# Retention attention and a gated feed-forward in one kernel: sums, casts, loads, stores and quarter products in another order

## The chip, the cores and the metric

The kernel runs on one core of a Trainium2 chip. The core has a matrix engine (TensorE, PE in the profile, with PEld for its weight loads), three engines for element-wise work (VectorE or DVE, ScalarE or ACT, GpSimd or POOL), and SyncE (SP), whose queue issues almost all transfers here. Each engine runs its own queue of instructions in the order in which the program wrote them; between engines they wait for each other by semaphores. The metric is the device time of one execution in microseconds (us). The kernel of before took 303.46 us, the median of 3 runs from 302.69 to 303.69.

## The reference

Inputs are q, k and v of 8 batches, 8 heads, 576 positions and 64 elements, and three weights of a feed-forward from 512 to 1536 and back. All are float32.

```python
gamma = 1.0 - 2.0 ** (-5.0 - np.arange(H))
Dmat = np.where(rel >= 0, gamma[:, None, None] ** rel[None, :, :], 0.0)   # rel = pos[:, None] - pos[None, :]
scores = scale * np.matmul(q, k.transpose(0, 1, 3, 2))
attn = np.matmul(scores * Dmat[None], v)
x = attn.transpose(0, 2, 1, 3).reshape(B * S, H * D)                      # 4608 tokens of 512
gate = 1.0 / (1.0 + np.exp(-(x @ w_gate)))
val = x @ w_val
out = gate * val @ w_out
```

The decay in Dmat allows the attention to be computed in pieces of 128 positions: within a piece by scores and a mask, and from earlier pieces through a state of 64 by 64 per head.

## The kernel before, in words

**Stages.** The 4608 tokens are the columns of a transposed activation `xT`. They are cut into blocks: 512 columns, two blocks of 256, and seven of 512, from column 1024 to column 4096. While the feed-forward of one block runs, the attention that makes the next blocks' columns is woven in, step by step. There are some 26 attention steps. Step s has loads of k, q and v (`load`, line 165, on SP), casts with decay tables to bf16 (`cast_qk`, `cast_v`, lines 420 to 445, on POOL, ACT or DVE; `SCALED_V`, `K_ON_POOL`, `V_ON_ACT` choose), a transposing DMA from SBUF to SBUF (`cross`, line 446, on SP) that makes the tile `T` of the step, and the products on PE (`row`, `new`, `val`, lines 686 to 734). Before PE's result `val` is cast into `xT`, a short read of it (`glance`, lines 753 and 755, on ACT or DVE by `LOOK_ACT`) makes the engine wait for it.

**How loads are ordered.** `casts_to(x)` first calls `loads_to(x + AHEAD[x])`, then writes the casts of step x and its transposing DMA. `AHEAD` thus sets how many steps' loads stand ahead of the transpose in SP's queue.

**Feed-forward of the first three blocks.** The first 512 columns and the two blocks of 256 use plain products: 128 columns of a weight by up to 512 columns of `xT`. Some of them are given to PE in two halves of 256 columns: how many is set by `CUTS` (line 1359), `FIRST_OP_CUTS` (line 1539) and `OP_CUTS` (line 1297).

**Feed-forward from column 1024 on.** Each block multiplies a 2 by 2 arrangement by seven products instead of eight (Strassen's scheme in Winograd's form), once for the gate (g), once for the value (w) and for each of three thirds u of the 1536 columns. A name such as `w14` means kind w, third u = 1, product i = 4. One product is four matmuls of 128 by 256. It needs sums of weights (`wgt`, `wvt`, `wvt_last` and so on; `w_sums`, line 359, `wo_sums`, line 318) and sums of tokens (`xsum`, four per block; `x_sums`, line 959). Its results leave PSUM through `quarter` (line 1052): product 1 is copied by ACT into `gateg`/`wg`, onto which product 2 is accumulated, products 5 and 6 into `gs`/`ws` and `gu`/`wu`, to which DVE adds products 7 and 3 (lines 1088 and 1085), and each finished quarter is made into `gv`, by the sigmoid on ACT for the gate, by a multiplication on DVE or POOL for the value (lines 1071 and 1073). Each kind and third has three PSUM buffers, a, g and e (in the profile `gatea`, `gateg`, `gatee`, `wa`, `wg`, `we`), which other thirds use again in turn; `BANKS`, line 1005, says which. The down projection is done by seven products too (`quarters`, line 1140, results `qa`, `qe`, `qf`); it needs sums of `gv`, called `gsum` (`gv_sum`, line 938).

**What sets the order.** The schedule is written out by hand. The strings `FIRST` (column 1024), `ORDER` (1536 to 3584, five blocks) and `FINAL` (4096) give the order of the quarter products on PE, and with it that of their followers on ACT, DVE and POOL. A suffix `:1-1v` behind a product says that at this place a `gsum` is written, on DVE (v) or POOL (p). `LATER_FIRST`, `LATER` and `LATER_FINAL` do the same at numbered places of the down projection. `X_LATE` says which engine makes each of the four `xsum` of a block from column 1536 on (the order is xsum_0 first half, xsum_1 first half, xsum_0 second half, xsum_1 second half, which product 4 reads). `SUMS_AT` does the same for the weight sums and the casts of the first stages: `2.12:w12p` writes the sum for w, third 1, number 2 on POOL at place 12 of block 2; a `c` is a cast step. `SOONER` and `CASTS_AT` place three stores and two cast steps in block 2.

The block at column 1024 has a special end: its last third of the value is done with plain products (`value`, line 1098, `h`, line 1106), the first of each in two halves.

## Time and profile before

| what | value |
|---|---|
| median of 3 runs | 303.46 us (302.69 to 303.69) |
| the profiled execution | 303.89 us |
| its span in the trace | 302.2 us |
| granted TensorE clock, mean | 0.999 |
| DMA packets | 146464, 54.99 MB |

The span is the part that the trace shows; 1.7 us lie around it. PE starts its first real products near 12 us and its last near 298 us. Before lie loads, casts and transposes; after, the last results are copied by DVE and stored.

The share of the span by which an engine is busy is in the page's first part. The chain that ended last is followed back from the last instruction: at each step to what released it, or to the instruction ahead of it on its engine. In a timeline row stand the start in us, the duration in us, engine, line, operation, output and inputs, shape and type, and in brackets the engine's idle time before it with what ended it. PE's rows are recorded from the issue of a matmul to the modelled end of its pipeline, so neighbours overlap: the distance between starts is what a product costs PE, 0.436 us for four matmuls of 128 by 256.

### The profile page before, as it was taken

To read this page: it belongs to the slowest core of one execution; us is meant where nothing else is said; L and a number is where in the kernel's file an instruction comes from. 1 tells how busy PE (TensorE), PEld (TensorE's weight loads), DVE (VectorE), ACT (ScalarE), POOL (GpSimd) and SP (SyncE) were. 2 spreads that over 40 slices of the span, in tenths; PEclk is the share of its full clock that TensorE was granted. 3 is DMA by queue.
4 is the path that set the end of the run, shared out by engine and by line. 5 is a ranking of instruction groups with operands and counts; after the bars stand their busy time and mean duration, and the time that the engine had idled before them with its cause. 6 is when DMAs were issued, how large, how long until landed. Compare 5 with 4: busy or idle time off the path is not lost.

```text
span 302.2 us, 10696 instructions
## 1 busy us (share of the span) xinstructions
PE 295.6 (98%) x4437; PEld 250.0 (83%) x4437; DVE 230.4 (76%) x439; ACT 204.9 (68%) x414; POOL 225.8 (75%) x253
## 2 busy tenths in 40 slices
PE   7999999999999999999999999999999999999994
PEld 3677876978868888888888888888888888888883
DVE  5967895796986998789748974896489848935893
ACT  6755565335369657985798589857985698559830
POOL 5775854846669888978997898789978946860780
PEclk9999999999999999999999999999999999999999
DMA  7999999979998989999749967976694165004013
GB/s 205 336 370 379 322 334 229 210 160 202 213 175 184 257 173 196 219 201 262 141 108 199 259 143 155 218 185 143 124 204 132 37 123 193 4 2 139 3 36 104
DMA packets 146464, 54.99 MB, mean 182 GB/s; under 512 B 124400, under 2 KB 139760, under 8 KB 146416
## 3 DMA queue, kind: packets, MB, share of 16 engines
q1 hardware_dynamic: 145328, 53.59, 73.6%
q8 instruction: 34, 0.56, 0.8%
q10 hardware_dynamic: 1088, 0.72, 0.8%
q14 instruction: 14, 0.11, 0.1%
HBM read 37.75 MB, written 9.44 MB: 156 GB/s over the span
## 4 chain that ended last, share of the span: by engine, by line
PE 92%; DVE 2%; DMA 2%; issue 1%; ACT 1%; POOL 0%; SPq 0%; DVEq 0%
PE gatea L1046 12%; PE wa L1046 11%; PE qa L1173 11%; PE qe L1173 9%; PE gatee L1046 6%; PE we L1046 5%; PE op L1549 4%; PE h_v L886 3%; PE h_g L886 3%; PE gateg L1046 3%; PE wg L1046 3%; PE hv L1374 3%; PE op L1306 3%; PE val L718 2%; PE qa L1249 2%; PE hg L1374 2%
## 5 line engine op out<-in xcount | busy, mean ns | idle before, releaser
L1046 PEld LDWEIGHTS <-wg_sb 128*128 128x128 bf16 x348 | 34.1, 98 | 4.1
L1073 POOL TENSOR_TENSOR gv<-gv,wu 128x512 bf16<-128x512 bf16 x20 | 23.5, 1174 | 15.5 <-DVE wu L1085 15.4
L1173 PEld LDWEIGHTS <-gsum 128*128 128x128 bf16 x312 | 30.0, 98 | 3.7
L429 POOL TENSOR_TENSOR qk<-q,qtab 128x512 bf16<-128x512 f32 x28 | 30.3, 1082 | 3.5 <-DMA q<-in_q_dram 3.5
L1046 PEld LDWEIGHTS <-wv_sb 128*128 128x128 bf16 x296 | 28.9, 98 | 3.6 <-issue 0.2
L1085 DVE TENSOR_TENSOR gu<-gatee,gu 128x512 f32<-128x512 f32 x22 | 15.2, 690 | 19.4 <-ACT gateg L1077 10.2
L943 POOL TENSOR_TENSOR gsum<-gsum,gv 128x256 bf16<-128x256 bf16 (+1 forms) x20 | 17.6, 890 | 14.4 <-DVE gsum L943 12.6
L1046 PEld LDWEIGHTS <-wgt_sb 128*128 128x128 bf16 x264 | 25.8, 98 | 3.0
L1046 PE MATMUL gatea<-xsum,wg_sb 128*128 128x256 bf16 x172 | 25.6, 273 | 0.0
L1173 PEld LDWEIGHTS <-gv 128*128 128x128 bf16 x228 | 21.8, 98 | 2.7
L1088 DVE TENSOR_TENSOR gs<-gatea,gs 128x512 f32<-128x512 f32 x22 | 15.2, 689 | 9.5 <-PE gatea L1046 9.4
L943 POOL TENSOR_TENSOR gsum<-gv,gsum 128x256 bf16<-128x256 bf16 (+1 forms) x24 | 21.9, 922 | 0.2
L429 POOL TENSOR_TENSOR qk<-k,ktab 128x512 bf16<-128x512 f32 x11 | 11.6, 1054 | 13.4 <-DMA k<-in_k_dram 13.2
L704 DVE TENSOR_TENSOR pt<-row,tri 128x512 bf16<-128x512 f32 x30 | 19.2, 680 | 2.8 <-PE row L686 2.6
L442 POOL TENSOR_TENSOR v<-v,ktab 128x512 bf16<-128x512 f32 x19 | 20.9, 1101 | 0.0
L1046 PE MATMUL wa<-xsum,wv_sb 128*128 128x256 bf16 x136 | 20.4, 273 | 0.1
L658 ACT CAST sb<-s 128x512 bf16<-128x512 f32 (+1 forms) x26 | 14.3, 569 | 8.8 <-DVE s L829 8.7
L788 ACT CAST xT<-val 128x512 bf16<-128x512 f32 x26 | 14.7, 592 | 7.0 <-PE val L734 7.0
L943 DVE TENSOR_TENSOR gsum<-gv 128x512 bf16<-128x512 bf16 (+1 forms) x34 | 19.1, 589 | 0.0
L1046 PEld LDWEIGHTS <-wvt 128*128 128x128 bf16 x168 | 16.4, 98 | 1.9
L943 POOL TENSOR_TENSOR gsum<-gv 128x256 bf16<-128x256 bf16 (+1 forms) x20 | 17.6, 882 | 0.0
L1071 ACT ACTIVATE gv<-gs 128x512 bf16<-128x512 f32 x22 | 13.9, 633 | 5.4 <-DVE gs L1088 5.4
(210 smaller groups left out, 883.9 us busy)
## 6 DMA issues: line engine op xcount, KB each, us to landing
k<-in_k_dram SPq DMA_DIRECT2D x26, 256.0 KB, 3.9
q<-in_q_dram SPq DMA_DIRECT2D x26, 256.0 KB, 4.2
v<-in_v_dram SPq DMA_DIRECT2D x26, 256.0 KB, 4.6
out_dram<-ob SPq DMA_DIRECT2D x24, 256.0 KB, 2.7
wg<-in_moe_w_gate_dram SPq DMA_DIRECT2D x12, 256.0 KB, 5.4
wv<-in_moe_w_val_dram SPq DMA_DIRECT2D x12, 256.0 KB, 5.6
wo<-in_moe_w_out_dram SPq DMA_DIRECT2D x12, 256.0 KB, 5.6
v32p<-in_v_dram SPq DMA_DIRECT2D x6, 256.0 KB, 4.5
```

The source lines that it names most:

```text
L429: eng.tensor_tensor(out=to, in0=by_halves(loaded[s][1 - i]), in1=tab, op=ALU.mult)
L442: nc.gpsimd.tensor_tensor(out=natural["v", s], in0=loaded[s][2], in1=tab, op=ALU.mult)
L704: nc.vector.tensor_tensor(out=t[:, y, 0:n].rearrange("p i m t -> p (i m) t"), in0=rows_tile[ss[0]][y][:, 0:n].rearrange("p i m t -> p (i m ...
L788: nc.scalar.copy(out=to, in_=src)
L886: nc.tensor.matmul(ps[:, i], lhsT=w_sb[:, kc, (fc + i) * P:(fc + i + 1) * P], rhs=xT(kc, slice(t0, t0 + n)), start=(kc == 0), stop=(kc == ...
L943: eng.tensor_tensor(out=to, in0=a, in1=b, op=op)
L1046: nc.tensor.matmul(ps[:, f], lhsT=w[:, kc, f * P:(f + 1) * P], rhs=x[:, kc], start=(first and f == 0 and kc == 0), stop=(f == 1 and kc == ...
L1073: eng.tensor_tensor(out=to, in0=to, in1=src[:, part], op=ALU.mult)
L1085: nc.vector.tensor_tensor(out=me["u2"], in0=e, in1=me["u2"], op=ALU.add)
L1088: nc.vector.tensor_tensor(out=me["s5"], in0=a, in1=me["s5"], op=ALU.add)
L1173: nc.tensor.matmul(ps[:, b], lhsT=left(fp)[:, b * P:(b + 1) * P], rhs=right(fp), start=(first and fp == 0 and b == 0), stop=(fp == NFC // ...
L1374: nc.tensor.matmul(ps[:, cols], lhsT=(wg_sb if what == "g" else wv_sb)[:, kc, fc * P:(fc + 1) * P], rhs=xT(kc, cols), start=(kc == 0), sto ...
```

## The change

No instruction's work changes. What changes is where it stands in a queue, which of two engines does it, and for seven pairs of matmuls whether they are one of 512 columns or two of 256.

```diff
-    X_LATE = "ppvp"
+    X_LATE = 'ppvv'
...
-    K_ON_POOL = (13, 15, 17, 18, 19, 22, 26, 27, 28, 29)
-    V_ON_ACT = ()
+    K_ON_POOL = (7, 12, 13, 15, 17, 19, 21, 22, 23, 27, 28, 29)
+    V_ON_ACT = (14,)
...
-    AHEAD = (2, 2, 1, 1, 0, 1, 1, 0, 1, 2, 1, 1)
+    AHEAD = (2, 2, 1, 1, 0, 1, 1, 1, 2, 3, 0, 1)
...
-    FIRST = ("g01 g11 g05 w05 g06 g15 g03 w01 g02 g16 g12 g07 w06 g13 g21 g17 w03 w11 w07 g04 g14 w02 w04 "
-             "w16 w12 g26:0-1v w15:0-2v:0-3p w17 g25 g22 w13 g27:0-4v g23 w14:1-1v v8:1-2p v9:1-3v g24 v10 "
-             "v11:2a1v:2a2p:2b1v:2b2p").split()
+    FIRST = ("g01 g11 g05 w05 g06 g15 g03 w01 g02 g16 g12 w06 g07 g13 g17 g21 w03 w11 w07 g14 g04 w02 w04v "
+             "w16 g26 w12:0-1v w15:0-2v:0-3p w17 g25 w13 g22 g27:0-4v g23 w14:1-1v:1-3v v8:1-2p v9 g24 v10 "
+             "v11:2a1v:2a2v:2b1v:2b2p ").split()
...
-    ORDER = ("g02 g06 g11 w05 g03 g15 w01 g07 g16 g12 w06 g13 w02 g21 g17 w11 w03 w07v g22 g04 g26 w04 "
-             "g25:0a1v:0b1v w16:0a2p:0b2p g14 w12 w15:0a4p:0b3p:0b4p w21 g27:0a3p w17 w13 w22 w26 w25 g23 "
-             "w27 w14 w23 g24 w24:1-1v").split()
+    ORDER = ("g02 g06 g11 w05 g03 g15 w01 g07 g16 g12 w06 g13 w02 w03 g21 w11 g17 w07v g22 g04 g26 w04 "
+             "g25:0a1v:0b1v w16:0a2p:0b2p w12:0a3v g14 w15:0a4p:0b3p:0b4p w21 g27 w17 w13 w22 w26v w25 g23 "
+             "w27 w14 g24 w23 w24:1-1v ").split()
...
-    OP_CUTS = (6, 11, 0, 0)
+    OP_CUTS = (3, 11, 0, 0)
...
-    CUTS = 60
+    CUTS = 59
...
-    FIRST_OP_CUTS = 20
+    FIRST_OP_CUTS = 16
...
-               "1.13:t07v 1.16:o23v 1.17:c08v 2.1:g22v 2.3:o22v 2.6:o13v 1.5:g02v 2.12:w12p "
-               "2.22:o02p 2.39:o12v 3.2:w20v 3.2:w21v 3.3:w23v 3.9:w22v").split()
...
+               "1.5:g02v 1.6:g12v 1.8:w02v 1.10:o21v 1.12:c09v 1.13:t07v 1.13:g22v 1.16:o23v 2.5:c08v 2.6:o22v "
+               "2.6:o13v 2.13:o02p 2.15:w12p 2.39:o12v 3.2:w20v 3.2:w21v 3.4:w23v 3.9:w22p ").split()
...
-    SOONER = (-14, -21, 12)
+    SOONER = (-12, -20, 10)
```

Left out are the other entries of `SUMS_AT`, and `LOOK_ACT`, `CASTS_AT`, `LATER_FIRST`, `LATER`, `LATER_FINAL` and `PAIRS_AT`, which are changed in the same manner. Some entries come out as they were: `CUTS` (48 cuts are used), the last entry of `PAIRS_AT`, `V_ON_ACT`, the 7 in `K_ON_POOL`, the v behind w02, w04 and w26.

The first place is SP's queue near the end of the blocks of 256 columns. The number behind a name only counts tiles; `k_9` to `v_12` are the loads of the steps, and `T_1937` (now `T_1945`) is the transpose of step 8, `T_1959` (now `T_1967`) that of step 9. Before:

```order
L171 DMA v_9_1932<-in_v_dram 128x8x64
L448 DMA_TRANSPOSE T_1937<-qk_1934 128x8x128
L171 DMA k_10_1941<-in_k_dram 128x8x64
L171 DMA q_10_1943<-in_q_dram 128x8x64
L171 DMA v_10_1945<-in_v_dram 128x8x64
L174 DMA k_11_1947<-in_k_dram 64x8x64 x2
L174 DMA q_11_1950<-in_q_dram 64x8x64 x2
L174 DMA v_11_1953<-in_v_dram 64x8x64 x2
L448 DMA_TRANSPOSE T_1959<-qk_1956 128x8x128
L913 DMA out_dram<-ob_1119 128x512
```

And now:

```order
L171 DMA v_9_1934<-in_v_dram 128x8x64
L171 DMA k_10_1936<-in_k_dram 128x8x64
L171 DMA q_10_1938<-in_q_dram 128x8x64
L171 DMA v_10_1940<-in_v_dram 128x8x64
L448 DMA_TRANSPOSE T_1945<-qk_1942 128x8x128
L174 DMA k_11_1949<-in_k_dram 64x8x64 x2
L174 DMA q_11_1952<-in_q_dram 64x8x64 x2
L174 DMA v_11_1955<-in_v_dram 64x8x64 x2
L171 DMA k_12_1958<-in_k_dram 128x8x64
L171 DMA q_12_1960<-in_q_dram 128x8x64
L171 DMA v_12_1962<-in_v_dram 128x8x64
L448 DMA_TRANSPOSE T_1967<-qk_1964 128x8x128
```

The three loads of step 10 moved ahead of the transpose of step 8, those of step 12 ahead of the transpose of step 9.

The second place is POOL's queue at the start of the block at column 1024: the cast of v of step 9, a token sum, casts of step 10, weight sums (`wv_sb`, `wo_sb`) and the first products of gate and value (`gv`). Before:

```order
L444 CAST v_1961<-v_9_1932 128x512
L970 TENSOR_TENSOR xsum_1_2159<-xT_1963,xsum_0_2158 128x512
L365 TENSOR_TENSOR wv_sb<-wv_sb 128x2x256
L429 TENSOR_TENSOR qk_2251<-k_10_1941,ktab_249 128x2x4x64
L429 TENSOR_TENSOR qk_2251<-q_10_1943,qtab_248 128x2x4x64
L444 CAST v_2256<-v_10_1945 128x512
L1073 TENSOR_TENSOR gv_0_2150<-gv_0_2150,wu_1024_0_2243 128x2x256
L1073 TENSOR_TENSOR gv_0_2150<-gv_0_2150,ws_1024_0_2187 128x2x256
L324 TENSOR_TENSOR wo_sb<-wo_sb 128x2x256
L943 TENSOR_TENSOR gsum_0_1_2332<-gv_0_2150 128x512
```

And now:

```order
L444 CAST v_1969<-v_9_1934 128x512
L970 TENSOR_TENSOR xsum_1_2158<-xT_1920,xsum_0_2157 128x512
L324 TENSOR_TENSOR wo_sb<-wo_sb 128x2x256
L429 TENSOR_TENSOR qk_2255<-k_10_1936,ktab_249 128x2x4x64
L429 TENSOR_TENSOR qk_2255<-q_10_1938,qtab_248 128x2x4x64
L444 CAST v_2260<-v_10_1940 128x512
L365 TENSOR_TENSOR wv_sb<-wv_sb 128x2x256
L1073 TENSOR_TENSOR gv_0_2149<-gv_0_2149,wu_1024_0_2235 128x2x256
L1073 TENSOR_TENSOR gv_0_2149<-gv_0_2149,ws_1024_0_2185 128x2x256
L943 TENSOR_TENSOR gsum_0_1_2330<-gv_0_2149 128x512
```

The weight sum `wo_sb` moved from behind the two `gv` to ahead of the casts of step 10, and `wv_sb` from ahead of those casts to behind them.

The third place is ACT's queue in the block at column 1536, the first of the five that follow `ORDER`, from the activation of `gu_1536_1` (product g13's sum) to the sigmoid of `gateg_2`, which frees the buffer that g25 fills, and the one behind it. Before:

```order
L1071 ACTIVATE gv_1_2930<-gu_1536_1_2978 128x2x256
L1077 COPY gateg_2_3009<-gatea_2_3004 128x512
L1071 ACTIVATE gv_1_2930<-gs_1536_1_2958 128x2x256
L1077 COPY wg_1_3022<-wa_1_3016 128x512
L1071 ACTIVATE gv_2_3003<-gateg_2_3009 128x2x256
L1071 ACTIVATE gv_0_2884<-gatea_0_2885 128x2x256
```

And now:

```order
L1071 ACTIVATE gv_1_2922<-gu_1536_1_2970 128x2x256
L1077 COPY gateg_2_3007<-gatea_2_3001 128x512
L1077 COPY wg_1_3014<-wa_1_3009 128x512
L1071 ACTIVATE gv_1_2922<-gs_1536_1_2950 128x2x256
L1071 ACTIVATE gv_2_3000<-gateg_2_3007 128x2x256
L1071 ACTIVATE gv_0_2877<-gatea_0_2878 128x2x256
```

The activation of `gs_1536_1`, to which product g17 is added, moved behind the copy of `wa_1` (product w11). The other four blocks of `ORDER` have the same rows.

More of the change, by code (lines that the diff above doesn't have):

```diff
@@ L431 @@
     SCALED_V = 11
-    X_LATE = "ppvp"
-    X_FIRST = "vvvp"
-    LOOK_ACT = (0, 5, 6, 9, 10, 13, 14, 17, 18, 19, 20, 21, 22, 25, 26, 27, 29, 33, 34)
-    K_ON_POOL = (13, 15, 17, 18, 19, 22, 26, 27, 28, 29)
-    V_ON_ACT = ()
+    X_LATE = 'ppvv'
+    X_FIRST = 'vvvp'
+    LOOK_ACT = (5, 6, 10, 11, 13, 14, 15, 17, 18, 19, 20, 21, 22, 26, 27, 28, 29, 30, 33, 34)
+    K_ON_POOL = (7, 12, 13, 15, 17, 19, 21, 22, 23, 27, 28, 29)
+    V_ON_ACT = (14,)
     def cast_v(s, eng):
@@ L1595 @@
     casts_to(1)
-    SUMS_AT = ("0.0:c03p 0.1:f00p 0.3:g00p 0.3:w10v 0.3:w11v 0.6:t01p 0.7:o10p 0.8:c02v "
[3 rows of a table removed]
-               "2.22:o02p 2.39:o12v 3.2:w20v 3.2:w21v 3.3:w23v 3.9:w22v").split()
+    SUMS_AT = ("0.0:c03p 0.2:f00p 0.3:g00p 0.3:w10v 0.3:w11v 0.7:t01p 0.7:o10p 0.8:c04p 0.9:o00v 0.11:c05p "
+             "0.11:c07p 0.12:w13v 0.12:c06v 0.14:g01v 0.14:g03p 0.15:c02v 1.0:o20v 1.3:o11p 1.4:o01v 1.5:o03v "
+             "1.5:g02v 1.6:g12v 1.8:w02v 1.10:o21v 1.12:c09v 1.13:t07v 1.13:g22v 1.16:o23v 2.5:c08v 2.6:o22v "
+             "2.6:o13v 2.13:o02p 2.15:w12p 2.39:o12v 3.2:w20v 3.2:w21v 3.4:w23v 3.9:w22p ").split()
     sums_at = {}
@@ L1609 @@
             w_sums(k, i, u, eng))
-    PAIRS_AT = ((0, 10), (0, 11), (1, 10), (1, 0))
+    PAIRS_AT = ((0, 10), (0, 11), (1, 10), (1, 2))
     paired = 0
-    SOONER = (-14, -21, 12)
+    SOONER = (-12, -20, 10)
     pieces = 0
```

12 lines of the change are left out of this document (6 added, 6 removed), and 2 rows, old and new, of the table SUMS_AT.

## The prediction

> **What bounds the kernel.** I read the page first: how full each engine is, and which one carries the chain that ended last.
>
> ```profile
> PE 295.6 (98%) x4437; PEld 250.0 (83%) x4437; DVE 230.4 (76%) x439; ACT 204.9 (68%) x414; POOL 225.8 (75%) x253
> ...
> PE 92%; DVE 2%; DMA 2%; issue 1%; ACT 1%; POOL 0%; SPq 0%; DVEq 0%
> ```
>
> PE is full. The change takes almost nothing from PE, so it can gain only where PE waits for another engine. A view by stretches shows the stretch in which five like blocks begin; its columns are the stretch, its length, then busy time and instructions of PE, PEld, DVE, ACT and POOL, the granted clock, DMA share and GB/s.
>
> ```profile
> 118.00:150.00 32.00, 32.00 (x519) 28.52 (x517) 27.69 (x51) 24.77 (x50) 28.90 (x30) 1.00 1.03 199
> ```
>
> PE runs at full clock (1.00) and looks busy without a break. But busy time hides short waits, because a matmul's recorded time runs on after its successor could have started. The chain of waits shows the longest of them, in columns start, length and who had the chain:
>
> ```profile
> 65.95 0.41 ACT sb L658
> ...
> 102.66 0.69 DVE ws L1088
> 103.35 0.04 issue
> 103.39 0.60 PE wa L1046 x4
> 103.99 1.74 PE h L1106 x14
> 105.73 0.44 PE gatea L1046 x4
> 106.17 1.85 PE h L1106 x14
> ```
>
> At 66 us PE waits for ACT's cast of the state; the diff leaves that wait alone. At 103.39 product w14 of the block at column 1024 waits for DVE's `ws` (line 1088), which stood behind two slow sums on line 943. The timeline there:
>
> ```profile
> 98.89 1.16 POOL L1073 TENSOR_TENSOR gv<-gv,ws 128x512 bf16<-128x512 bf16 x1
> ...
> 99.89 0.69 DVE L1073 TENSOR_TENSOR gv<-gv,wg 128x512 bf16<-128x512 bf16 x1
> ...
> 100.00 1.16 POOL L324 TENSOR_TENSOR wo_sb<-wo_sb 128x512 bf16<-128x512 bf16 x1
> ...
> 100.49 0.95 DVE L943 TENSOR_TENSOR gsum<-gv 128x512 bf16<-128x512 bf16 x1
> ...
> 101.12 1.34 POOL L943 TENSOR_TENSOR gsum<-gv 128x512 bf16<-128x512 bf16 x1
> ...
> 101.48 1.26 DVE L943 TENSOR_TENSOR gsum<-gsum,gv 128x512 bf16<-128x512 bf16 x1
> ...
> 102.74 0.60 PE L1046 MATMUL gatee<-xT,wgt_sb 128*128 128x256 bf16 x4
> ...
> 104.46 0.41 DVE L943 TENSOR_TENSOR gsum<-gv,gsum 128x512 bf16<-128x512 bf16 x1
> ...
> 105.39 0.67 DVE L1073 TENSOR_TENSOR gv<-gv,wa 128x512 bf16<-128x512 bf16 x1
> ```
>
> One product occupies PE for 0.436 us (the chain has 1.74 for four products' worth of columns, line 1106). After the start at 102.74 the next was due at 103.18, and it came at 103.39: 0.21 us lost. In the second half of the last products in this block (line 1106) the chain has 1.85 us for 14 pieces, where the first half has 1.74: 0.11 lost, behind DVE's `gv<-gv,wa`, which ended at 106.06. Adding up all such gaps between starts from 30 to 298 us, I find about 0.9 us that another order could give back, 0.30 of it at 66 us and a few pieces of 0.1 to 0.2 behind glances at attention results. **The most that this change can gain is therefore some 0.9 us, 0.3%**, about what a measurement of this kernel can tell from no change.
>
> **The change, part by part.**
>
> *Fewer halves.* Seven pairs of 256-column matmuls become one 512-column matmul each. What halves cost is in the chain:
>
> ```profile
> 20.69 1.74 PE hg L1374 x14
> ...
> 82.00 1.73 PE op L1306 x8
> ```
>
> The first is 4096 columns in 14 pieces (two whole, twelve halves), the second 4096 columns in 8 whole ones. Six more pieces cost at most 0.01 us, so seven fewer save 0.01 to 0.02: **−0.02**. The Trainium skill, page "TensorE: Matmul & The Clock Gate", section "Back-to-back issue gap", gives a sustained 131 ns for a 512-column matmul; by that seven pairs would save 0.6 us (an estimate from that page against 0.218 for two halves here). The trace disagrees, with 1.73/8 = 0.216 us, and decides.
>
> *Loads ahead of the transpose, and POOL's sums* (column 1024). SP now issues the loads of step 10 before the transposing DMA, not after it.
>
> ```profile
> 84.53 0.90 SPq L171 DMA_DIRECT2D q<-in_q_dram  x1
> ...
> 86.92 4.11 SPq L448 DMA_TRANSPOSE T<-qk  x1
> ...
> 91.17 1.04 POOL L429 TENSOR_TENSOR qk<-q,qtab 128x512 bf16<-128x512 f32 x1 [2.54 <-DMA q<-in_q_dram]
> ```
>
> The page gives such a load from issue to landing, in the median:
>
> ```profile
> q<-in_q_dram SPq DMA_DIRECT2D x26, 256.0 KB, 4.2
> ```
>
> The q that POOL wants was issued at 84.53, and by the median of 4.2 us it would land at 88.7. It landed near 91.1, with the transpose set going in between, and POOL stood 2.54 us. With the transpose behind three more loads, POOL gains between 0 (the DMA engines were merely full) and 2.4 us (88.7 for 91.1); I take 1.6, nearer the median landing, since three loads now share the engines. POOL also gets the `wo_sb` sum (1.16) into this chain, ahead of its two `gv` adds; before, it came after them. They end at 98.89 + 1.16 = 100.05 now and at 100.05 + 1.16 − 1.6 = 99.6 after; with no gain at 101.2. At 99.6 POOL's own `gsum` (1.34) runs before 101.3, and DVE's two sums, which follow `gv<-gv,wg` of a product that is now given one slot later (99.89 becomes 100.3, to 101.0), run mostly alone, at 0.41 as at 104.46. They end near 101.8 instead of 102.7, `ws` near 102.5, and w14 at 103.2 waits for nothing: **−0.21**. The DVE chain behind it comes forward as well, so the wait before the last products goes: **−0.11**. What is late next there is PE itself. The transposes of steps 8 and 9, each now behind three loads, are first read by PE here:
>
> ```profile
> 109.65 0.47 PE L686 MATMUL row<-T 64*64 64x64 bf16 x31
> ```
>
> The first was issued 22.7 us before that (at 86.92), so two or three us of delay cost nothing; the second has half of that.
>
> *Products one place apart* in the first block. g17 goes ahead of g21. It fills the buffer that ACT empties last:
>
> ```profile
> 94.37 0.59 ACT L1025 COPY gu<-gatea 128x512 f32<-128x512 f32 x1
> ...
> 94.88 0.60 PE L1046 MATMUL gatea<-xT,wg_sb 128*128 128x256 bf16 x4
> ...
> 95.32 0.49 PE L1046 MATMUL gatea<-xsum,wg_sb 128*128 128x256 bf16 x3
> ```
>
> g17 starts at 95.32; now its turn is 94.88, and the copy ends at 94.96 plus a hop (0.04 in the chain): **+0.12**. The cost lies between 0, if ACT comes forward by as much, and 0.44, a whole slot. The other swaps (w06 with g07, g14 with g04, w12 with g26, w13 with g22) exchange products whose buffers were free at least about 0.1 us before; I take 0, with up to 0.1 each way for two of them.
>
> *The five blocks from 1536 to 3584.* w03 goes from behind w11 to ahead of g21, so g17 comes two slots later. The trace of the first of them:
>
> ```profile
> 126.76 1.04 POOL L429 TENSOR_TENSOR qk<-q,qtab 128x512 bf16<-128x512 f32 x1
> 126.79 0.68 DVE L1073 TENSOR_TENSOR gv<-gv,wg 128x512 bf16<-128x512 bf16 x1
> ...
> 127.38 0.68 DVE L1088 TENSOR_TENSOR gs<-gatea,gs 128x512 f32<-128x512 f32 x1
> ...
> 127.61 0.60 PE L1046 MATMUL we<-xT,wvt 128*128 128x256 bf16 x4
> ...
> 128.10 0.63 ACT L1071 ACTIVATE gv<-gs 128x512 bf16<-128x512 f32 x1
> ...
> 129.52 0.60 ACT L1071 ACTIVATE gv<-gateg 128x512 bf16<-128x512 f32 x1
> ...
> 129.64 1.16 DVE L1073 TENSOR_TENSOR gv<-gv,ws 128x512 bf16<-128x512 bf16 x1
> ...
> 130.23 0.60 PE L1046 MATMUL gatee<-xsum,wgt_sb 128*128 128x256 bf16 x4
> ```
>
> The product at 130.23 (g25) needs the sigmoid at 129.52 done, at 130.12: 0.10 us to spare. After: g17 runs from 127.61 to 128.21, DVE's `gs` from 128.25 to 128.93, ACT's activation of `gs` (0.63) to about 129.6 and the sigmoid, which stands behind it, to 130.2. That is 0.05 to spare, and **0** is my term. It is open on both sides: +0.1 in each block if every hop is a little longer; nothing below 0, since PE lost nothing here before. POOL is relieved of a quarter of its token sums (`xsum`) and some `gsum` work, which DVE takes on:
>
> ```profile
> L970 DVE TENSOR_TENSOR xsum<-xT,xsum 128x512 bf16<-128x512 bf16 x7 | 6.8, 970 | 1.0 <-POOL xsum L970 0.9
> ...
> L943 DVE TENSOR_TENSOR gsum<-gv 128x256 bf16<-128x256 bf16 x12 | 3.5, 332 | 0.0
> ```
>
> That is 0.97 + 0.33 us of DVE per block, where DVE is busy 27.69 of 32 us. The moved `xsum` is first read by the block's twenty-first product (g04), some twenty times 0.436 us after its first, so PE feels it only if DVE's queue backs up. In the block at 1536 it may: a weight sum also moves ahead of `gs` there, so `gs` can be up to 0.6 us late. The cost is 0 to 0.4, once; I take 0, because the product that reads its result comes later still.
>
> *The rest.* Casts between POOL and ACT, the glances and the final block move work on engines with idle time, off PE's path. The last PE work and the closing store, 298.0 to 302.2, stay as they are.
>
> **Sum:** −0.21 − 0.11 − 0.02 + 0.12 = −0.22 us. The profiled execution took 303.89 us (302.2 of span and 1.7 around it), so 303.67 on its own terms. It stands 0.43 above the median of the runs, 303.46; from that the sum gives 303.24, or **303.2 us**.
>
> **Rivals.**
>
> *POOL is not early* (27%). If the q lands late because the DMA engines are full, POOL's adds end at 101.2, DVE's two sums start there beside POOL's `gsum` and take 0.95 and 1.26 again, `ws` ends near 104.1, and w14 waits 0.9. Against 0.21 now that is +0.7, and with the g17 term +0.8: **304.3**. With half the gain (0.8) the waits stay as they are, and the time is 303.5 to 303.7. For it: the DMA engines are full in much of the program (share 1.03 in the stretch shown above, which begins later). Against it: the 4.2 us median.
>
> *The five blocks lose the chain to g25* (13%), the slower case. It decides at one point: whether DVE starts `gs` by 128.3. Ahead of it now stand `gv<-gv,wg` and `wu`. If the first takes 1.16, as `gv<-gv,ws` does at 129.64, instead of 0.68, then `wu` ends at 128.64, `gs` at 129.32, the sigmoid near 130.6, and g25 waits 0.37: 5 × 0.37 = +1.9, **305.1**; at half of that 304.2. Against it: POOL was at work beside the 0.68 as well. The Trainium skill, page "SBUF — State Buffer", section "Who interferes with whom", says that a VectorE instruction with two SBUF inputs contends with a GpSimd instruction that reads SBUF; where the lock is taken, the first holds it for the whole instruction. The 0.97 mean of DVE's `xsum` beside 0.41 for a lone sum agrees; the 0.68 at 126.79 does not show it.
>
> *More goes than I see* (8%). If the glances and small waits also vanish, all 0.9 us goes: **302.6**.
>
> *The change does less than it says* (10%). Only seven of the halves change, and several entries of the tables name a product or cast that comes out the same. If the moved DMA and sums shift waits without moving PE, it is **303.4**.
>
> **How the numbers follow.** The forecast has 42%, with 302.9 to 303.5 as its own range. Slower by over 0.3% (above 304.37) takes 6 points of the 13 of the five blocks, 5 of the 27 of a late POOL and 2 for several small waits at once: 0.13. Faster by over 0.3% (below 302.55) is most of the third rival: 0.07. The range runs from 302.5, all stalls gone, to 304.4, POOL not early at all.
>
> **What would show it.** POOL's `qk<-q` of step 9 starts near 89.4, not 91.2; w14 starts 0.44 us after the product before it; the two `gsum` on DVE ahead of it take about 0.4 each; g17 shows a gap near 0.1 behind ACT's copy; g25 follows its neighbour by 0.44 in all five blocks. Wrong would be a gap before g25 that recurs with each block, a w14 that waits more than 0.2, or a PE whose starts are as dense as forecast while the time still moves, which would mean that the head or the closing store changed.

## The result, and the profile after

The changed kernel took 306.06 us, the median of 7 runs from 305.07 to 306.62. The kernel before, run beside it, took 303.55 us (7 runs, 302.69 to 305.03). The ratio is 1.0073, with an interval from 1.0047 to 1.0098: the change made the kernel slower, by some 2.5 us. The forecast was 303.2 us with a range up to 304.4. The profiled execution, 306.62 us with a span of 304.9 at a granted clock of 1.0, was the slowest of the seven, and that matters below.

The page of the changed kernel, its first part (busy time and share of each engine) and the chain that ended last by engine:

```profile
PE 296.8 (97%) x4430; PEld 249.4 (82%) x4430; DVE 235.9 (77%) x452; ACT 204.2 (67%) x413; POOL 217.4 (71%) x241
...
PE 93%; DVE 2%; DMA 1%; issue 1%; ACT 1%; POOL 0%; SPq 0%; DVEq 0%
```

PE is still the bound, with 7 matmuls fewer, and the work went from POOL to DVE as the diff says. Nothing here shows where 2.7 us of span came from. For that I set the start of the same product in both traces side by side, from stage to stage:

| stretch | changed less before, us | what is late there |
|---|---|---|
| up to the block at column 1024 | −0.28 | the start of the execution |
| block at 1024, feed-forward | +1.40 | w14, and g17 |
| block at 1024, down projection | +0.11 | one attention step |
| blocks from 1536 to 2560 | +0.48 | 0.27 of it at w11 and g22 of the first |
| attention in the down projection of 3072 | +0.56 | a wait with no releaser |
| from there to the last matmul | +0.01 | |
| after the last matmul | +0.38 | the end of the program |

The sum is 2.66, the difference of the spans but for rounding. Three places carry most of it; the blocks from 1536 on follow further below.

**w14.** The chain that ended last, in order of time (start, length, who had it):

```profile
94.77 0.99 PE gatea L1046 x8
...
102.37 0.45 PE gatea L1046 x4
...
102.97 0.81 issue
103.78 0.69 DVE ws L1088
104.47 0.04 issue
104.51 0.60 PE wa L1046 x4
```

From 102.37 to 104.51 stand two products, 2.14 us for twice 0.436: 1.27 us are lost, where it was 0.21 before. The releaser is again DVE's `ws`. The first row is g17: 0.99 for two products, 0.12 more than 0.87. DVE's timeline, and POOL's (start, duration, engine, line, operation, and in brackets the idle time before it with what ended it):

```profile
102.14 0.42 DVE L943 TENSOR_TENSOR gsum<-gv 128x512 bf16<-128x512 bf16 x1 [1.29 <-POOL gv L1073]
102.60 1.26 DVE L943 TENSOR_TENSOR gsum<-gsum,gv 128x512 bf16<-128x512 bf16 x1
103.78 0.68 DVE L1088 TENSOR_TENSOR ws<-wa,ws 128x512 f32<-128x512 f32 x1
```

```profile
91.00 1.04 POOL L429 TENSOR_TENSOR qk<-k,ktab 128x512 bf16<-128x512 f32 x1 [2.86 <-DMA k<-in_k_dram]
...
99.83 1.16 POOL L1073 TENSOR_TENSOR gv<-gv,wu 128x512 bf16<-128x512 bf16 x1
100.95 1.16 POOL L1073 TENSOR_TENSOR gv<-gv,ws 128x512 bf16<-128x512 bf16 x1
```

POOL was late, not early: it stood 2.86 us for k of step 9, its second `gv` ended at 102.11, and DVE had to wait for it. SP's queue says why:

```profile
84.14 0.92 SPq L171 DMA_DIRECT2D k<-in_k_dram  x1
85.10 0.94 SPq L171 DMA_DIRECT2D q<-in_q_dram  x1
...
92.69 2.39 SPq L448 DMA_TRANSPOSE T<-qk  x1
```

The k issued at 84.14 landed at 90.84, 6.7 us later, although the transpose of step 8 went out only at 92.69. So a load can be that late without a transpose in between. Whether that is the rule is asked below, with all profiles together.

**The attention in the down projection of 3072.** The chain there, first of the changed kernel, then of the one before:

```profile
232.99 0.09 PE val L734 x7
233.08 0.53 issue
233.60 0.26 PE val L734 x8
```

```profile
231.28 0.31 PE val L734 x16
```

In the middle of 16 small matmuls of one line PE stops for half a microsecond, and no semaphore ended the stop. By the starts it is 0.69 us, against 0.14 before.

**The end.** The last rows of both chains, before and changed:

```profile
298.31 0.42 DVE ob L1293
```

```profile
300.59 0.42 DVE ob L1293
```

From the end of DVE's last copy to the end of the span (302.24 and 304.90) it is 3.51 us before and 3.89 now. What lies there is the last stores and the closing instructions of each queue.

### The profile page after: what moved, and what is told of

It reads as the page before. It is cut to its first block, busy times and chain, and to the rows that moved or that the text cites. A ratio compares the mean times of both kernels' runs of the same rounds, so it can differ in the third digit from the quotient of the medians.

```text
span 304.9 us, 10687 instructions
## 1 busy us (share of the span) xinstructions
PE 296.8 (97%) x4430; PEld 249.4 (82%) x4430; DVE 235.9 (77%) x452; ACT 204.2 (67%) x413; POOL 217.4 (71%) x241
## 4 chain that ended last, share of the span: by engine, by line
PE 93%; DVE 2%; DMA 1%; issue 1%; ACT 1%; POOL 0%; SPq 0%; DVEq 0%
PE gatea L1046 13%; PE wa L1046 12%; PE qa L1173 11%; PE qe L1173 9%; PE gatee L1046 6%; PE we L1046 6%; PE op L1549 3%; PE gateg L1046 3%; PE h_v L886 3%; PE h_g L886 3%; PE wg L1046 3%; PE hv L1374 3%; PE op L1306 3%; PE val L718 2%; PE qa L1249 2%; PE hg L1374 2%
## 5 line engine op out<-in xcount | busy, mean ns | idle before, releaser
L943 POOL TENSOR_TENSOR gsum<-gsum,gv 128x256 bf16<-128x256 bf16 (+1 forms) x18 | 15.6, 876 | 18.4 <-DVE gsum L943 17.8
L943 DVE TENSOR_TENSOR gsum<-gv 128x512 bf16<-128x512 bf16 (+1 forms) x39 | 21.8, 582 | 1.3 <-POOL gv L1073 1.3
L943 POOL TENSOR_TENSOR gsum<-gv,gsum 128x512 bf16<-128x512 bf16 (+1 forms) x23 | 21.4, 939 | 1.3 <-DVE gsum L943 1.2
L1073 POOL TENSOR_TENSOR gv<-gv,ws 128x512 bf16<-128x512 bf16 x14 | 16.3, 1163 | 2.9 <-DVE ws L1088 2.3
```

What stands on the lines that cost most here:

```text
L943: eng.tensor_tensor(out=to, in0=a, in1=b, op=op)
L1073: eng.tensor_tensor(out=to, in0=to, in1=src[:, part], op=ALU.mult)
```

## The experiments

The runs came in three groups; each group has its own runs of the kernel before. The expectations call theories by letters; what each is about stands in the words around them.

### First group: which part of the change costs it

The first theory was that w14 is the whole loss, and the suspects were the two sums that POOL does earlier, the loads, and the five blocks. Three kernels undo one part of the change each, the fourth does one alone.

`pool_back`, the changed kernel with POOL's two sums where they were:

```diff
-             "2.6:o13v 2.13:o02p 2.15:w12p 2.39:o12v 3.2:w20v 3.2:w21v 3.4:w23v 3.9:w22p ").split()
+             "2.6:o13v 2.12:w12p 2.22:o02p 2.39:o12v 3.2:w20v 3.2:w21v 3.4:w23v 3.9:w22p ").split()
```

> The changed kernel with only two weight sums put back on POOL: o02 behind the two gv of the block at column 1024, w12 ahead of the casts of step 10. Theory P (POOL's chain): in the changed kernel POOL's second gv ends at 102.11 us, of which 1.15 is the o02 sum in front of it; DVE's two gsum wait for it and w14 waits 1.25 us behind them. P expects gv to end near 101.0, the wait before w14 to fall to 0.1 to 0.6 us, and the time to fall by 0.6 to 1.1 us, to some 305.2. Rival B (the five like blocks cost the time): no change, 306.1, though the wait at w14 may be shorter. Rival L (the loads put ahead of the transpose cost it): no change of w14's wait beyond 0.3.

`loads_back`, the changed kernel with the loads where they were:

```diff
-    AHEAD = (2, 2, 1, 1, 0, 1, 1, 1, 2, 3, 0, 1)
+    AHEAD = (2, 2, 1, 1, 0, 1, 1, 0, 1, 2, 1, 1)
```

> The changed kernel with only AHEAD as before, so the transposes of steps 8 and 9 stand ahead of the loads of steps 10 and 12 again. Theory P: the q of step 9 lands 6.6 us after its issue with or without the transpose in between (6.6 in both traces), so the time stays within 0.4 us of 306.1 and POOL's wait for step 9 stays 2 to 3 us. Rival L (the order of loads costs the time): 0.8 to 2 us faster, and POOL's chain at the block's start earlier by as much. Theory F, on which the forecast was made (the transpose delays the loads): 1 us or more slower.

`blocks_back`, the changed kernel with `X_LATE`, `ORDER` and `LATER` of before:

```diff
-    X_LATE = 'ppvv'
+    X_LATE = "ppvp"
...
-    ORDER = ("g02 g06 g11 w05 g03 g15 w01 g07 g16 g12 w06 g13 w02 w03 g21 w11 g17 w07v g22 g04 g26 w04 "
+    ORDER = ("g02 g06 g11 w05 g03 g15 w01 g07 g16 g12 w06 g13 w02 g21 g17 w11 w03 w07v g22 g04 g26 w04 "
...
-    LATER = {0: ('2-1v', '2-2p'), 1: ('1-2v',), 2: ('2-3p',), 4: ('1-3v',), 5: ('1-4p',), 10: ('2-4p',)}
+    LATER = {0: ('2-1v',), 1: ('1-2v', '2-2p'), 2: ('2-3p',), 4: ('1-3v',), 9: ('1-4p',), 10: ('2-4p',)}
```

> The changed kernel with ORDER, LATER and X_LATE as before, so the five blocks from column 1536 (and the xsum of the last) run as before. Theory P: the trace of the changed kernel shows about 0.3 us of waits in these blocks that were not there (0.09 and 0.19 in the first, 0.1 in others), so 0.2 to 0.6 us faster, some 305.6. Rival B (a wait that recurs in each block): 1.5 to 2.5 us faster, near 304.

`pool_alone`, the kernel before with POOL's two sums where the change puts them:

```diff
-               "1.13:t07v 1.16:o23v 1.17:c08v 2.1:g22v 2.3:o22v 2.6:o13v 1.5:g02v 2.12:w12p "
-               "2.22:o02p 2.39:o12v 3.2:w20v 3.2:w21v 3.3:w23v 3.9:w22v").split()
+               "1.13:t07v 1.16:o23v 1.17:c08v 2.1:g22v 2.3:o22v 2.6:o13v 2.13:o02p 2.15:w12p 1.5:g02v "
+               "2.39:o12v 3.2:w20v 3.2:w21v 3.3:w23v 3.9:w22v").split()
```

> The kernel of before with only the two sums moved as in the change: o02 ahead of the casts of step 10 on POOL, w12 behind them. Theory P: POOL's two gv end 1.1 us later, DVE's gsum follow, and w14 waits about 1.1 to 1.3 us where it waited 0.21: 0.8 to 1.1 us slower, near 304.5. Rivals B and L: within 0.4 us of before, 303.5.

The kernel before took 303.79 us in this group (29 runs).

| kernel | median, us (runs) | ratio to before, interval |
|---|---|---|
| pool_back | 305.29 (7) | 1.0040 [1.0023, 1.0058] |
| loads_back | 305.03 (11) | 1.0049 [1.0032, 1.0066] |
| blocks_back | 304.79 (12) | 1.0036 [1.0020, 1.0053] |
| pool_alone | 303.94 (12) | 0.9994 [0.9976, 1.0012] |

`pool_alone` costs nothing: the two sums ahead of POOL's `gv` do not make w14 late by themselves. Its POOL timeline has them in between, and the second `gv` still ends at 100.59, 1.5 us sooner than in the changed kernel, where POOL had stood for k:

```profile
93.34 1.15 POOL L324 TENSOR_TENSOR wo_sb<-wo_sb 128x512 bf16<-128x512 bf16 x1
...
97.19 1.16 POOL L365 TENSOR_TENSOR wv_sb<-wv_sb 128x512 bf16<-128x512 bf16 x1
98.31 1.16 POOL L1073 TENSOR_TENSOR gv<-gv,wu 128x512 bf16<-128x512 bf16 x1
99.43 1.16 POOL L1073 TENSOR_TENSOR gv<-gv,ws 128x512 bf16<-128x512 bf16 x1
```

Three kernels that undo three different things all stay 1.0 to 1.5 us slower, and in none of their profiles did w14 wait; the longest wait in that block is 0.25 us, in `loads_back`. So w14 does not explain the loss of the median, and no one of the three parts does. What all three share with the changed kernel is the wait in the attention of 3072 (0.51, 0.74 and 0.81 us), and an end that is 0.21 to 0.39 us longer than before. All three also have the changed kernel's seven fewer halves, and `pool_alone` has not; in it the wait is gone. This made the next theory: **PE waits there for its own instructions.**

### Second group: the halves, and the changed kernel again

The page's third part lists what brings instructions. Before:

```profile
q8 instruction: 34, 0.56, 0.8%
```

These are 34 packets, 0.56 MB together, 16 KB each. PE has 4437 matmuls, as many weight loads and three more: 8877 instructions. 0.56 MB over 8877 instructions are 63 bytes each; with 64, 16 KB are 256 instructions, so one packet would bring one **block of 256 instructions** to PE. The Trainium skill, page "Runtime: NRT & Kernel Launch", section "Instruction fetch mechanics", states that an engine's instructions are refilled in 16 KiB blocks of 256; the packets here agree. It also holds the cost of crossing such a boundary to be mostly hidden; this case has a place where it is not.

The wait stands at PE's instruction number 7103 in every kernel that has it, whatever instruction that is. 7103 is 191 + 27 × 256, and from 191 on the 8877 instructions make 33.9 such blocks, for 34 packets. With seven pairs merged, 14 instructions are gone ahead of it (a matmul and a weight load each), so the block up to the boundary lies 14 instructions later in the program. Before, 227 of its 256 instructions belong to the small matmuls of the attention; now 241 do, and PE runs through them faster. (The expectation of `cuts_alone` calls this place the end of the block at column 3584; it is that of 3072.)

`cuts_alone`, the kernel before with the halves of the changed kernel, and nothing else:

```diff
-    OP_CUTS = (6, 11, 0, 0)
+    OP_CUTS = (3, 11, 0, 0)
...
-    FIRST_OP_CUTS = 20
+    FIRST_OP_CUTS = 16
```

> The kernel of before with only the seven pairs of halves made whole (FIRST_OP_CUTS 16, OP_CUTS 3), which is 14 PE instructions fewer. Theory I (instruction blocks): PE's instructions are fetched in blocks of 16 KB, 256 of them; in all traces so far PE stops at its instruction number 7103, in the attention at the end of the block at column 3584, whatever stands there. 14 instructions fewer put that place 14 deeper into a stretch of small matmuls, and leave the fetch less time. It expects the wait there to grow from 0.14 to between 0.5 and 0.8 us and the time to rise by 0.4 to 0.7 us, to some 304.2. Rival D (that wait comes from the order of DVE's and ACT's work in the change): wait as before, time within 0.2 us of before, as the forecast had it (0.02 us faster).

`cuts_back`, the changed kernel with the halves of before:

```diff
-    OP_CUTS = (3, 11, 0, 0)
+    OP_CUTS = (6, 11, 0, 0)
...
-    FIRST_OP_CUTS = 16
+    FIRST_OP_CUTS = 20
```

> The changed kernel with only the seven pairs given in halves again, as before. Theory I: the wait at PE's instruction 7103 falls from 0.5 to 0.8 us to 0.2 or less, and the time by 0.4 to 0.7 us against the changed kernel, to 305.4 (by medians of the same call). Rival D: wait and time stay as in the changed kernel.

`cuts_blocks_back` has the edits of `cuts_back` and `blocks_back` together:

```diff
-    X_LATE = 'ppvv'
+    X_LATE = "ppvp"
...
-    OP_CUTS = (3, 11, 0, 0)
+    OP_CUTS = (6, 11, 0, 0)
...
-    FIRST_OP_CUTS = 16
+    FIRST_OP_CUTS = 20
```

> The changed kernel with the halves and the five like blocks both as before. If the two costs add (0.5 and about 0.4 us) and the wait at w14 is only an accident of when k and q of step 9 land, the time is 303.8 to 304.5, within 0.3% of before, with what is left from the closing of the engines' queues (0.2 to 0.35 us) and g17 (0.12). Rival S (something else in the change costs a microsecond): 305 or more.

`after_again` is the changed kernel unaltered.

> The changed kernel once more, unaltered, to see how often its wait before w14 comes. Theory P': it comes when k and q of step 9 land after 90.5 us and POOL, with the o02 sum ahead of its gv adds, ends these after 101; so the runs fall in two groups about 1.1 us apart, near 305.2 and 306.3, and the profile has either the whole wait or next to none. Rival: one group around 306, with the wait in every profile.

The kernel before took 303.67 us in this group (30 runs).

| kernel | median, us (runs) | ratio to before, interval |
|---|---|---|
| after_again | 305.17 (7) | 1.0059 [1.0038, 1.0080] |
| cuts_back | 304.67 (12) | 1.0033 [1.0017, 1.0049] |
| cuts_blocks_back | 303.93 (12) | 1.0013 [0.9993, 1.0034] |
| cuts_alone | 304.61 (12) | 1.0031 [1.0015, 1.0046] |

Merging seven pairs, alone, costs 0.94 us (0.46 to 1.40 by the interval). The chain of `cuts_alone` and that of `cuts_back` at the place:

```profile
231.46 0.09 PE val L734 x7
231.55 0.92 issue
232.47 0.26 PE val L734 x8
```

```profile
231.56 0.16 PE val L734 x15
231.72 1.42 PE qe L1173 x12
```

With the halves back the small matmuls run through in 0.16 us; with the halves merged and nothing else they stop. The records of the transfers let the theory be tested in each run: when PE passes the instruction 256 ahead of the boundary, when the packet of the block runs, and when PE goes on.

```
kernel            PE instr.  PE at 6847  packet runs       PE at 7103  wait   PE's own time  packet's end to PE
before               8877      228.38    228.30 - 229.70     231.27    0.14       2.75            1.57
pool_alone           8877      228.85    228.39 - 229.95     231.58    none       2.73            1.63
order_alone          8877      227.85    227.12 - 228.66     230.58    none       2.73            1.92
xsum_alone           8877      228.36    227.98 - 229.58     231.09    none       2.73            1.51
cuts_back            8877      228.67    228.51 - 229.38     231.40    none       2.73            2.02
cuts_blocks_back     8877      228.04    228.30 - 229.31     230.93    0.12       2.77            1.62
more_halves          8895      228.68    229.32 - 230.41     232.30    none       3.62            1.90
best                 8895      227.05    227.76 - 228.69     230.68    none       3.62            1.98
after                8863      230.86    231.37 - 232.26     233.60    0.69       2.05            1.35
after_again          8863      229.38    229.60 - 230.48     232.05    0.61       2.05            1.57
pool_back            8863      229.57    229.81 - 230.69     232.13    0.51       2.05            1.44
loads_back           8863      230.31    230.12 - 231.64     233.10    0.74       2.05            1.46
blocks_back          8863      228.88    228.99 - 230.30     231.77    0.81       2.07            1.47
cuts_alone           8863      229.34    229.33 - 230.93     232.47    1.08       2.05            1.54
```

(Four of the rows belong to the third group, below. The wait is the distance between the starts of two matmuls, less the time of the first.) The packet starts within 0.75 us of PE passing instruction 6847, takes 0.9 to 1.6 us, and PE goes on 1.35 to 1.62 us after its end wherever it had to wait. From one boundary to the next PE has 2.73 to 2.77 us of work with the alignment of before, and the block is there just in time; with 14 instructions fewer it has 2.05 us, and PE waits in all six profiles of the five kernels. That is the cause of the wait at 7103, shown by doing it alone, by undoing it, and by the times of the packets. The length of the packet is also in the view of transfers, over 4 us at the place (packets, MB, share of 16 engines), before and changed:

```profile
q8 instruction: 1, 0.02, 2.2%
```

```profile
q8 instruction: 1, 0.02, 1.4%
```

2.2% of 16 engines over 4 us are 1.41 us, and 1.4% are 0.90: the packet was even shorter in the changed kernel. By its end it came 1.3 us after PE had passed 6847 before the change and 1.4 us after it now: PE was early, not the packet late.

`after_again` settled a second point. In its profiled execution (305.07 us, span 303.3) w14 does not wait at all. Its SP queue and its POOL, for the rows shown above:

```profile
80.67 1.11 SPq L171 DMA_DIRECT2D k<-in_k_dram  x1
81.82 1.75 SPq L171 DMA_DIRECT2D q<-in_q_dram  x1
...
87.78 2.63 SPq L448 DMA_TRANSPOSE T<-qk  x1
```

```profile
85.58 1.04 POOL L429 TENSOR_TENSOR qk<-k,ktab 128x512 bf16<-128x512 f32 x1
...
98.65 1.16 POOL L1073 TENSOR_TENSOR gv<-gv,ws 128x512 bf16<-128x512 bf16 x1
```

The same program issued k of step 9 at 80.67 here and at 84.14 in the other execution, where SP's issues of v and of the next k took 2.2 to 2.4 us each. POOL cast it at 85.58 instead of 91.00, and ended its second `gv` at 99.81 instead of 102.11. From stage to stage this execution stands against before as follows: −0.19 at the start, −0.06 in the block at 1024, +0.50 in the blocks from 1536 to 2560, +0.45 in the attention of 3072, +0.40 at the end: 1.10, the difference of the spans. So the wait of w14, 1.3 us, belongs to the execution, and the rest, 1.1 to 1.4, to the program. The 14 runs of the changed kernel lie at 304.19, at 305.00 to 305.42 (6), and at 305.86 to 306.62 (7), and the one profile with the wait is from the last group, the one without from the middle. That would fit a load that is late in half of them; two profiles don't show it.

### Third group: the five blocks, and one more shift

With halves and blocks both undone the time is 0.26 us above before, and the interval includes no change at all. Undoing the blocks as well was worth 0.74 us (304.67 to 303.93). Which of their edits? In `cuts_back` the chain shows the one wait that they have in common, at g22 of the block at 1536:

```profile
127.14 0.52 PE wa L1046 x4
127.66 0.44 PE gatea L1046 x4
128.10 0.44 PE wa L1046 x4
128.53 0.02 issue
128.56 0.60 PE gateg L1046 x4
```

g22 stands behind w07 there and comes 0.19 us late by the starts, and w11, 0.52 for a product in the chain, 0.08; in the changed kernel's ACT timeline it is released by a copy that stands behind an activation:

```profile
128.80 0.65 ACT L1071 ACTIVATE gv<-gu 128x512 bf16<-128x512 f32 x1
129.33 0.61 ACT L1077 COPY gateg<-gatea 128x512 f32<-128x512 f32 x1
```

The copy ends at 129.94, and g22 starts at 129.99. ACT has no idle time from 126.84 on, so the delay is older. DVE's and ACT's rows ahead of it in the changed kernel, and DVE's in `blocks_back`, where neither w11 nor g22 waits:

```profile
124.92 1.29 DVE L365 TENSOR_TENSOR wvt_last<-wv_sb,wvt_last 128x512 bf16<-128x512 bf16 x1
126.13 0.68 DVE L1088 TENSOR_TENSOR gs<-gatea,gs 128x512 f32<-128x512 f32 x1
126.84 0.63 ACT L1071 ACTIVATE gv<-gs 128x512 bf16<-128x512 f32 x1 [0.55 <-DVE gs L1088]
```

```profile
123.30 0.44 DVE L365 TENSOR_TENSOR wvt_last<-wv_sb,wvt_last 128x512 bf16<-128x512 bf16 x1
123.93 0.69 DVE L1088 TENSOR_TENSOR gs<-gatea,gs 128x512 f32<-128x512 f32 x1 [0.19 <-PE gatea L1046]
```

The weight sum `wvt_last`, which the change moves to the place right ahead of `gs` (from ahead of `gu`), takes 1.29 us where it takes 0.44 with the blocks undone. `gs` is late by it, ACT stands 0.55 us, and everything behind in ACT's queue is late, down to the copy that frees g22's buffer.

`order_alone` is the kernel before with `ORDER` and `LATER` of the change:

```diff
-    ORDER = ("g02 g06 g11 w05 g03 g15 w01 g07 g16 g12 w06 g13 w02 g21 g17 w11 w03 w07v g22 g04 g26 w04 "
+    ORDER = ("g02 g06 g11 w05 g03 g15 w01 g07 g16 g12 w06 g13 w02 w03 g21 w11 g17 w07v g22 g04 g26 w04 "
...
```

> The kernel of before with only ORDER and LATER as in the change (w03 ahead of g21, one gsum to DVE, the later sums placed anew), the fourth xsum still on POOL. The changed kernel has two waits in the block at column 1536 that before had not: w11 for ACT's sigmoid (0.09 us) and g22 for ACT's copy of product g21 (0.19). Theory O (the new order of the products makes them): both are here, 0.2 to 0.4 us slower, 303.9 to 304.1. Rival X (the fourth xsum on DVE makes them): neither is here, time within 0.15 us of before.

`xsum_alone` is the kernel before with this:

```diff
-    X_LATE = "ppvp"
+    X_LATE = 'ppvv'
```

> The kernel of before with only X_LATE as in the change: the fourth xsum of six blocks on DVE, not POOL. Theory O: no new wait on PE in the five blocks, time within 0.2 us of before. Rival X: w11 and g22 wait 0.1 to 0.3 us at column 1536, 0.2 to 0.4 us slower.

`more_halves` is the kernel before with nine more pairs given out in halves, 18 more instructions on PE:

```diff
-    OP_CUTS = (6, 11, 0, 0)
+    OP_CUTS = (11, 11, 0, 0)
...
-    FIRST_OP_CUTS = 20
+    FIRST_OP_CUTS = 24
```

> The kernel of before with nine more pairs given in halves (FIRST_OP_CUTS 24, OP_CUTS 11 at its first place), 18 PE instructions more. Theory I: the block boundary at PE's instruction 7103 moves 18 instructions towards the start of the stretch of small matmuls, the fetch gets about 0.9 us more, and the wait there (0.14 to 0.16 in before) goes; by the halves themselves at most 0.02 us is added. Time 0 to 0.2 us faster than before. Rival H (halves cost by themselves what the seven gained): 0.5 us or more slower, or a wait at 7103 as in before or longer.

`best` is `cuts_blocks_back` with the same nine more halves, and with the glance of step 0 on ACT; against `cuts_blocks_back`:

```diff
-    LOOK_ACT = (5, 6, 10, 11, 13, 14, 15, 17, 18, 19, 20, 21, 22, 26, 27, 28, 29, 30, 33, 34)
+    LOOK_ACT = (0, 5, 6, 10, 11, 13, 14, 15, 17, 18, 19, 20, 21, 22, 26, 27, 28, 29, 30, 33, 34)
...
-    OP_CUTS = (6, 11, 0, 0)
+    OP_CUTS = (11, 11, 0, 0)
...
-    FIRST_OP_CUTS = 20
+    FIRST_OP_CUTS = 24
```

> The changed kernel with the five blocks as before, nine more halves than before, and the glance at the first attention result on ACT as before (one DVE instruction fewer). It keeps the new order of the first stages and of the block at column 1024, which in the traces without a late load gain some 0.15 us there. Theory I: no wait at 7103. Theory T (the closing of the engines' queues depends on how many instructions DVE and POOL have: 4.2 us from the last matmul with 571 on DVE, 4.4 with 572): the closing is 4.2 us again. Together 303.2 to 303.7, level with before or up to 0.4 us faster. Rival: 304 or more, if the order of the first stages costs time by itself.

The kernel before took 303.73 us in this group (35 runs).

| kernel | median, us (runs) | ratio to before, interval |
|---|---|---|
| order_alone | 303.98 (12) | 1.0013 [0.9992, 1.0034] |
| xsum_alone | 304.00 (12) | 1.0002 [0.9981, 1.0023] |
| more_halves | 304.36 (12) | 1.0028 [1.0005, 1.0051] |
| best | 304.88 (12) | 1.0025 [1.0002, 1.0047] |

Neither the order nor the `xsum` alone brings the wait at g22, and neither costs more than 0.34% at the end of its interval. Neither of the two has the moved weight sum, which comes from `SUMS_AT`; `blocks_back` has it and doesn't wait either. So the wait comes with that sum together with the new order, the `xsum` on DVE, or both; which wasn't settled.

`more_halves` did what was hoped at 7103: PE has 3.62 us of work up to the boundary and doesn't wait. But another boundary, at instruction 3519 = 191 + 13 × 256, now made it wait 0.68 us, in the down projection of 1024, and in `best` 0.33. The chain of `best` there:

```profile
114.91 1.42 PE qa L1173 x12
116.33 0.16 issue
116.49 1.47 PE qe L1173 x12
```

The packet of that block ran from 116.16 to 117.09 in `more_halves`, 1.6 us after PE had passed the instruction 256 ahead (114.58), and PE went on at 118.40, 1.31 us after its end. `xsum_alone`, with the alignment of before, had the same there: packet from 115.77, wait 0.35. `cuts_alone` has a second stop as well, of 0.4 us at instruction 5311 = 191 + 20 × 256, with 5 us of work ahead of it: its packet began 2.9 us after PE had passed the instruction 256 ahead, and PE went on 1.56 us after its end. So a packet can also start late, and moving the boundaries trades one such place for another. `best` was therefore not better than before. Its profiled execution was its fastest (303.34 us, span 301.7); its 12 runs reach up to 306.68, and what the slow ones have wasn't seen.

One wait in `cuts_alone` was of the kind of w14: ACT stood for a load of k, and behind it a copy for which PE waited 0.81 us at 181.31.

```profile
179.85 0.62 ACT L426 CAST qk<-k 128x512 bf16<-128x512 f32 x1 [1.19 <-DMA k<-in_k_dram]
```

No edit of that kernel lies near it, so a part of its +0.94 may be such a load, and a part the stop at 5311, which the changed kernel does not have. The price of the boundary at 7103 is therefore better read from its wait.

## Why the prediction was wrong, point by point

**Fewer halves, −0.02: the step that failed most.** That halves themselves cost next to nothing was right: `more_halves`, with 18 instructions more, lost 0.63 us, and its wait at the other boundary was 0.68. But the forecast took the change for seven matmuls at their own place. It also moved every later instruction of PE against the boundaries of the blocks of 256, and the boundary 7103 came 14 instructions deeper into a burst of small matmuls. That cost 0.94 us alone and gave 0.50 back when undone (305.17 to 304.67, with intervals that overlap); the wait itself is 0.5 to 1.1 us. No rival had it. The rows that could have led there were on the page of before, the 34 instruction packets, and in the trace, a stop of 0.14 us at 231.27 that no semaphore ended.

**Loads ahead of the transpose, −0.21 and −0.11: right about POOL in most executions, wrong about the gain.** The forecast put a load's late landing (84.53 to 91.1) down to the transpose in between. Over the fourteen profiles, q of step 9 took 5.4 to 6.6 us to land in all seven with the order of loads of before, and POOL's cast of it began at 88.4 to 91.4. With the new order it took 4.3 to 4.9 in five of seven, and the cast began at 86.0 to 87.7; in `pool_back` and in the first profile of the changed kernel it took 6.0 and 6.6, without a transpose in between. In these two SP also came to issue it late, at 84.5 and 85.1 instead of 81.3 to 82.5. So the order of the loads goes with the early POOL that was forecast, but does not ensure it; why SP is late in two wasn't settled.

The gain was a second matter. `cuts_alone`, `xsum_alone` and `more_halves` leave this part as it was, and in their profiles w14 waits for nothing and the second half of the last products takes 1.74, not 1.85. The 0.32 us that the two terms count on were a wait of the one execution that was profiled, and no saving where an execution has no such wait.

The two profiles of the changed kernel show both cases. In the second POOL is early, DVE's second sum takes 0.42 and w14 waits for nothing, as forecast; DVE's timeline of `after_again`:

```profile
101.65 0.42 DVE L943 TENSOR_TENSOR gsum<-gsum,gv 128x512 bf16<-128x512 bf16 x1
101.99 0.69 DVE L1088 TENSOR_TENSOR ws<-wa,ws 128x512 f32<-128x512 f32 x1
```

`ws` ends at 102.68, where the forecast had 102.5. In the first w14 lost 1.27, by the rival "POOL is not early", which had it wait 0.9. By the medians this place is not where most of the loss lies.

**g17, +0.12: right**, 0.99 for two products of 0.87 in both profiles.

**The five blocks, 0: a term that was named and taken as nothing.** The wait ahead of g25, which was the slower rival's point, came in none of the blocks. For the block at 1536 the forecast saw that a weight sum moves ahead of `gs` and makes it up to 0.6 us late, put the cost at 0 to 0.4, and took 0, because the product that reads the result comes later. ACT did stand 0.55 us for `gs`. The delay reached PE another way, through ACT's queue: the copies for w11 and g22 stand behind the activation of `gs`, and PE lost 0.27 us. The attention steps of the next blocks lost about 0.2 more. Undoing these edits brought 0.74 us (from 304.67 to 303.93), with two medians whose runs overlap; 0.15 of it is the end of the program. (Product g04, which reads the moved `xsum`, is the block's twentieth, not its twenty-first; nothing hangs on it.)

**The closing store "stays as it is": wrong, by 0.4 us.** From DVE's last copy to the end of the span it took 3.89 and 3.90 in the two profiles of the changed kernel, against 3.51 before. In the records of the changed kernel it is GpSimd's last DRAIN, which begins 0.3 us later and takes 188 ns instead of 40. The kernels differ in how many instructions DVE's queue holds: with 571 (five kernels, before and `best` among them) the end takes 3.49 to 3.53, with 572 (`blocks_back` and `cuts_blocks_back`) 3.72, with 583 (the changed kernel and three more) 3.86 to 3.90. But `xsum_alone`, with 577, takes 3.58 and `order_alone`, with 576, 3.76, so the count alone does not set it. The reason stays open.

**The account of the medians** is an estimate: some 0.5 to 0.9 us for the boundary, 0.4 to 0.7 for the five blocks, 0.2 to 0.4 for the end (a part of it is in the blocks' share too), less 0.1 to 0.3 in the first stages, and perhaps a late load in some executions, which the first measurement would have met more often than the second (306.06 and 305.17).

## What to carry to other kernels

In a program of thousands of instructions, look for stops of the bounding engine that no semaphore ends, and for what stands at their instruction numbers: if they lie a multiple of 256 apart, as 3519, 5311 and 7103 do here, adding or removing a few instructions anywhere ahead moves them into or out of a burst of short work. A transfer's landing time in one profile is no constant: before a forecast rests on it, look at when its queue issued it, and profile the same program twice; a wait that only one execution has is no gain to be had. Where the hoped gain is 0.2 us, a cost that the diff doesn't mention can be five times as large.

## What the runs showed of the hardware that was not expected

- PE's instructions come in packets of 16 KB for 256, one for each block, asked for about as PE reaches the block ahead. At the boundary 7103 the packet began within 0.75 us of that, took 0.9 to 1.6 us, and where PE waited, it went on 1.35 to 1.62 us after the packet's end. At other boundaries the packet began from 1.5 us before PE passed the instruction 256 ahead to some 4 us after. A block with 241 instructions of the small matmuls of the attention is done in 2.05 us, which is less than all that.
- Two executions of one program differed by 1.3 us at one product: in one the load of k was issued at 80.67 and landed 4.8 us later, in the other at 84.14 and 6.7 us later.
- A 256 KB load that the page gives as 4.0 to 4.7 us in the median took up to 6.7 us here, without a transposing DMA in between, and up to 6.6 us before, with one.
